# Spreading the router over the tiles of a window-attention + MoE kernel: two places a tile, one list product a part, an earlier second tile

## The chip, the core and the metric

One core of a Trainium2 chip runs the whole program. The metric is device time in microseconds, from the first to the last instruction of one execution plus what lies around it; lower is better. The engines are named as the profile names them: PE (TensorE matmul; PEld are its weight loads), DVE (VectorE), ACT (ScalarE), POOL (GpSimd), and SP, whose queue (SPq) issues most of the DMAs.

## What is computed

Attention over a window of 64 keys (8 batches, 8 heads, 576 positions, head size 64), and on its output a top-1 mixture of experts with a skip:

```
rel  = pos[:, None] - pos[None, :]
attn = softmax(where((rel >= 0) & (rel < 64), q @ k.T / 8, -1e9))
x    = (attn @ v) as [4608, 512]
do   = x @ w_skip > 0                      # other rows leave as x
e    = argmax(x @ w_gate); g = softmax(x @ w_gate)[e]     # 8 experts
out  = x + g * (relu(x @ w1[e]) @ w2[e])   # w1[e]: 512 x 1024
```

## The kernel before, in words

**Attention.** 36 tiles of 128 tokens go through a loop written out by hand (`for t in range(NT + 1)`, L868 to L894): inside `tc.manual_schedule()` every engine takes its instructions in program order. Turn t issues, in this order: loads that are due; `score(t+1)` (PE, L234); the gate matmuls of a coming v block (`gate_at`, PE and a copy on ACT); `soften(t)` (DVE: maximum L249, subtraction L250; then ACT: exponential L251); `tile_out(t-2)`, which is `av_tile` (PE L344, then on DVE the normalisation, L353 to L361) and two turns later a store; and `transpose_p(t-1)` (PE L260, ACT copy `ptm` L261). Scores sit in two PSUM buffers; the transposes, the gate matmuls and the router's own matmuls share another two (tag "t").

**Router.** Tiles are routed in groups of 8, 8, 6, 8, 4 and 2 (`GRP`). `route` is a generator: each `yield` ends a part. On DVE it reduces the logits (`lg`, L386), finds the winner (`gmx`, `gd`, `gfi`, `gfm`), builds a one-hot row (`goh`, `gohb`, after which it yields "sums"); then PE counts (`pr`, L410 and L413) and DVE goes on (`gds`, `base`, L422 and L423; `gnd`, `gs`, `gate`, `pos`, `low`, `posp`); then POOL writes one-hot positions (`hot`, L446), two tiles a part. `routes(n)` takes up to n parts; after "sums" it lets calls go by until the third, so that PE doesn't meet `gohb` too early. Before, a turn calls it at three places: ahead of `soften`, between normalisation and transposes, and after these (there with two parts from turn 22, `NCLOSE`, on).

**Lists.** When the third group is routed (22 tiles), `close_first` picks the two fullest experts, and `entries` makes their lists: DVE compares (`of`, L478), POOL multiplies it with five columns (`ofv`, L486, five products), PE sums (`pe`, L505), DVE turns it into indices (`entry`, L513 to L517), and POOL gathers the rows (`gather_x`, L524). The first item's rows are transposed (`split_x`, `px`, L684) in turns 32 and 33 (`XSPLIT`).

**Experts.** After the loop, `expert_chunk` issues one stretch of expert matmuls at a time (`up`: 12 matmuls and on ACT and DVE `hh`, `hl`; `down`: three wide matmuls a list tile and chunk; every fifth chunk is empty in the first items) and, ahead of it, the weight splits due (`whi` on ACT L647, `wlo` on DVE L648). While router parts are left, each chunk is followed by `routes(2)`. Then come `order_experts` (L952 on) and a loop that takes `PACE` parts of `late_lists` ahead of each chunk: `begins` (L969), then `entries` over nine steps of four tiles, with the matmuls (`peu`) two steps behind the products. Its list feeds the gather for the third item, whose transposes stand in the 29th chunk.

**Start.** SP loads q and k of the first two blocks, constants for the scores, `wg`, the first v (`load_v(0)`), q and k of blocks 2 and 3, the second q and k, and the router's constants (`load_constants`, `cf` and `cols`, with five small POOL instructions behind `cf`).

Of the kernel before, what the change touches and what calls it, by code (L numbers as in the profile page):

```python
# [13 lines left out]
ALU = mybir.AluOpType  # L14
# [5 lines left out]
P = 128  # L20
# [19 lines left out]
NCLOSE = 22  # L40
# [9 lines left out]
USPLIT = (35,)  # L50
RATE = 1

PACE = 4

XSPLIT = (32, 33)

# [68 lines left out]
def window_attention_moe(ctx: ExitStack, tc, a, out):  # L125
    nc = tc.nc
# [26 lines left out]
    vals = const.tile([P, 5, NT], BF16, name="vals")  # L153
# [31 lines left out]
    def load_qk(n, parts=((0, 4),)):  # L185
        b, g = divmod(n, 2)
        if parts[0][0] == 0:
            qs[n] = qkp.tile([P, 4, 4, 64], F32, name="q", bufs=NQB)
        q, k = qs[n], ks[n % NKB]
        for s, e in parts:  # L190
            s0 = s + 1 if s or not g else 0
            nc.sync.dma_start(k[:, s0 : e + 1], a["kT"][b, :, 4 * g + s0 - 1 : 4 * g + e])
            nc.sync.dma_start(q[:, s:e], a["qT"][b, :, 4 * g + s : 4 * g + e])
# [273 lines left out]
    def entries(ts, starts, le, pool, since, take, step, lag):  # L467


        nc_ = starts.shape[1]  # L470
        parts(slice(since, ts.stop))
        yield
        pe, built = None, []
        for t0 in range(ts.start, ts.stop, step):
            m = min(step, ts.stop - t0)
            tj = slice(t0, t0 + m)
            of = pool.tile([P, m, nc_], BF16, name="of", bufs=1 if take is psum else 3)
            nc.vector.tensor_tensor(  # L478
                of,
                posp[:, tj].unsqueeze(2).to_broadcast([P, m, nc_]),  # L480
                starts.unsqueeze(1).to_broadcast([P, m, nc_]),
                op=ALU.is_equal,
            )
            ofv = pool.tile([P, m, 5, nc_], BF16, name="ofv", bufs=1 if take is psum else 3)
            for v in range(5):
                nc.gpsimd.tensor_tensor(  # L486
                    ofv[:, :, v], of, vals[:, v, tj].unsqueeze(2).to_broadcast([P, m, nc_]), op=ALU.mult
                )
                if v in (1, 3):
                    yield  # L490
            built.append((t0, ofv))
            yield "sums" if take is psum else None
            if len(built) < lag and t0 + step < ts.stop:
                continue
            if pe is None:
                pe = (
                    psum.tile([P, 5, nc_], F32, name="pe", tag="t", bufs=2, padded_shape=[P, 5, 100])
                    if take is psum
                    else banks["late"].tile([P, 5, nc_], F32, name="peu", tag="u", bufs=1, padded_shape=[P, 5, 100])
                )  # L500
            while built and (len(built) >= lag or t0 + step >= ts.stop):
                first_t, ofs = built.pop(0)
                for j in range(ofs.shape[1]):
                    t = first_t + j
                    nc.tensor.matmul(pe, hot[:, t], ofs[:, j], start=t == ts.start, stop=t == ts.stop - 1)  # L505
                yield
        entry(pe, le, pool)
        yield
# [65 lines left out]
    held = [None, 0]  # L574

    def routes(n, sums=True):

        for _ in range(n):
            if not late:
                return  # L580
            if held[0] == "sums":
                held[1] += 1
                if not sums or held[1] < 3:
                    continue
            held[:] = next(late[0], late), 0
            if held[0] is late:
                late.pop(0)
# [52 lines left out]
    def weight_dma_first():  # L640
        weight_dma(ptr["dma"])
        ptr["dma"] += 1
# [189 lines left out]
    with tc.manual_schedule():  # L832
# [2 lines left out]
        nc.sync.dma_start(band, a["c_band"])  # L835
        load_qk(0, ((1, 2),))
        nc.sync.dma_start(ident, a["c_ident"])
        nc.sync.dma_start(wg, a["wg"])
        load_v(0)
        load_qk(0, ((2, 4),))  # L840
        load_qk(1)
        load_constants()
        at = {}

        def when_at(t, f, n):
# [22 lines left out]
        for t in range(NT + 1):  # L868
            m, r = divmod(t, 9)
            for f, n in at.get(t, ()):  # L870
                f(n)
            if t + 1 < NT:
                score(t + 1)
            for f, n in gate_at.get(t, ()):
                f(n)
            rest = its[0].split(*xhl[0], XSPLIT.index(t), "t") if t in XSPLIT else None
            routes(1)
            if t < NT:
                soften(t)
            if t >= 2 and t < NT:  # L880
                tile_out(t - 2)
            if rest is not None:
                rest()
            routes(1, False)
            if t >= 1 and t < NT:
                transpose_p(t - 1)
            routes(1 if t < NCLOSE else 2)
            for f, n, j in lower_at.get(t, ()):
                f(n, j)
            for _ in range(U0.count(t)):  # L890
                weight_dma_first()
            if t in USPLIT:
                weight_split(ptr["split"])
                ptr["split"] += 1  # L894
# [282 lines left out]
```

## Time and profile before

| | |
|---|---|
| median of 3 runs | 467.93 us (466.89 to 470.29) |
| the profiled execution | 465.82 us, span 464.0 us |
| busy share PE, DVE, ACT, POOL | 89%, 66%, 47%, 27% |
| mean granted TensorE clock | 0.975 of full |
| attention loop | to about 180 us |
| routing of the last groups and the late list, among the first expert chunks | about 183 to 238 us |
| rest of the experts | 238 to 464 us |

The shares are averages over stages with different limits: a busy PE near 89% includes 100 us in which it never rests and 32 us in which it rests a third of the time. How the stages stand is in the rows below.

### The profile page before, as it was taken

The numbers are of one execution on the slowest core, as the hardware profiler recorded it, in microseconds if no ns is written. First come the engines' busy times: TensorE is split into PE (matmuls) and PEld (weight loads), VectorE is DVE, ScalarE is ACT, GpSimd is POOL, SyncE is SP. The second block draws the span as 40 slices with busy tenths as digits, with TensorE's granted clock in tenths as the row PEclk, the third lists the DMA queues.
The fourth block names the chain that finished last, engine by engine and source line by source line (L and its number), as shares of the span: only waits on it lengthen the run. The fifth ranks groups of instructions, "written<-read, shape, count | busy, mean of one in ns | idle before, by whom it ended". The sixth has DMA issues, their size and how long they took to land.

```text
span 464.0 us, 11417 instructions
## 1 busy us (share of the span) xinstructions
PE 411.8 (89%) x4568; PEld 342.9 (74%) x4568; DVE 308.3 (66%) x609; ACT 218.4 (47%) x365; POOL 125.6 (27%) x188
## 2 busy tenths in 40 slices
PE   2899989979779967894899999999999999999983
PEld 2577767867567756783689888898888789988762
DVE  2478989989788988687533658947355566756420
ACT  1387667767546755462312534434243445444410
POOL 2311215116052505246860402405007030101010
PEclk9999999999898998996999999999999999999998
DMA  7999989949847943556533561845537456656100
GB/s 245 394 351 401 384 284 404 398 127 390 356 146 250 355 128 112 151 196 207 174 111 100 184 207 69 277 137 185 193 114 250 161 197 198 216 193 219 51 29 20
DMA packets 35096, 99.31 MB, mean 214 GB/s; under 512 B 4480, under 2 KB 6528, under 8 KB 35040
## 3 DMA queue, kind: packets, MB, share of 16 engines
q1 hardware_dynamic: 31840, 88.97, 55.8%
q0 software_dynamic: 3200, 9.58, 5.8%
q8 instruction: 37, 0.61, 0.5%
q14 instruction: 19, 0.16, 0.1%
HBM read 84.46 MB, written 14.39 MB: 213 GB/s over the span
## 4 chain that ended last, share of the span: by engine, by line
PE 64%; DVE 9%; ACT 3%; DMA 3%; POOL 2%; issue 1%; POOLq 0%; DVEq 0%; SPq 0%; ACTq 0%
PE p L695 8%; PE p L697 8%; PE p L696 8%; PE av L344 4%; PE yw L695 3%; PE yw L697 3%; PE yw L696 3%; PE yv L695 3%; PE yv L696 3%; PE yv L697 3%; PE pt L260 3%; PE ps L234 3%; POOL ofv L486 2%; DMA vm<-vp 2%; DVE s L250 2%; PE px L684 2%
## 5 line engine op out<-in xcount | busy, mean ns | idle before, releaser
L648 DVE TENSOR_TENSOR wlo<-raw,whi 128x1024 fp32r<-128x1024 f32 x72 | 88.1, 1229 | 15.4 <-ACT whi L647 15.4
L732 ACT ACTIVATE hh<-p 128x256 fp32r<-128x256 f32 (+6 forms) x72 | 27.7, 384 | 146.6 <-PE p L697 145.6
L697 PE MATMUL p<-xh,wlo 128*128 128x256 f32 (+6 forms) x288 | 84.2, 292 | 1.6 <-DVE wlo L648 1.6
L695 PE MATMUL p<-xh,whi 128*128 128x256 f32 (+6 forms) x288 | 85.3, 296 | 0.3 <-ACT ptm L261 0.3
L696 PE MATMUL p<-xl,whi 128*128 128x256 f32 (+6 forms) x288 | 84.1, 292 | 0.0
L733 DVE SCALAR_TENSOR_TENSOR hl<-p,hh 128x256 fp32r<-128x256 f32 (+6 forms) x72 | 30.3, 420 | 76.8 <-ACT hh L732 76.7
L647 ACT CAST whi<-raw 128x1024 fp32r<-128x1024 f32 x72 | 74.2, 1046 | 0.0
L755 POOL DMA_INDIRECT out<-yo,les x18 | 18.9, 1052 | 156.0 <-DVE yo L754 144.1
L695 PEld LDWEIGHTS p<-xh,whi 128*128 128x128 f32 x288 | 55.0, 191 | 3.4 <-ACT ptm L261 0.4
L251 ACT ACTIVATE s<-s 128x1024 f32<-128x1024 f32 x36 | 38.1, 1058 | 40.3 <-DVE s L250 38.1
L697 PEld LDWEIGHTS p<-xh,wlo 128*128 128x128 f32 x288 | 55.1, 191 | 2.0 <-DVE wlo L648 2.0
L696 PEld LDWEIGHTS p<-xl,whi 128*128 128x128 f32 x288 | 55.1, 191 | 1.4
L249 DVE TENSOR_REDUCE mx<-ps 128x8 f32<-128x1024 f32 x36 | 43.8, 1215 | 15.0 <-PE ps L234 15.0
L250 DVE TENSOR_TENSOR s<-ps,mx 128x1024 f32<-128x1024 f32 x36 | 44.1, 1225 | 5.1 <-PE pt L260 0.9
L260 PE MATMUL pt<-ident,s 128*128 128x128 f32 x288 | 41.0, 284 | 5.6 <-ACT ptm L261 5.6
L344 PEld LDWEIGHTS av<-vm,ptm 128*64 128x64 f32 x1024 | 36.1, 138 | 11.4 <-issue 5.7
L344 PE MATMUL av<-vm,ptm 128*64 128x74 f32 x1024 | 41.3, 233 | 2.2 <-ACT ptm L261 2.1
L315 POOL COPY vm<-vm 64x1184 f32<-64x1184 f32 x16 | 18.6, 1168 | 88.5 <-ACT vm L314 61.0
L234 PE MATMUL ps<-k,q 64*64 64x128 f32 x1024 | 37.3, 285 | 4.1 <-DMA q<-qT 4.1
L261 ACT COPY ptm<-pt 128x512 f32<-128x512 f32 x72 | 38.6, 580 | 4.7 <-PE pt L260 4.5
L260 PEld LDWEIGHTS pt<-ident,s 128*128 128x128 f32 x288 | 31.5, 143 | 9.8 <-ACT ptm L261 6.5
L234 PEld LDWEIGHTS ps<-k,q 64*64 64x64 f32 x1024 | 33.1, 142 | 7.2 <-DMA k<-kT 4.4
(173 smaller groups left out, 697.5 us busy)
## 6 DMA issues: line engine op xcount, KB each, us to landing
raw<-wq SPq DMA_DIRECT2D x72, 512.0 KB, 4.4
vm<-vp SPq DMA_DIRECT2D x16, 592.0 KB, 6.8
vT<-vT SPq DMA_DIRECT2D x16, 512.0 KB, 7.6
out<-x SPq DMA_DIRECT2D x32, 256.0 KB, 6.3
q<-qT SPq DMA_DIRECT2D x15, 512.0 KB, 9.0
k<-kT SPq DMA_DIRECT2D x8, 640.0 KB, 6.8
k<-kT SPq DMA_DIRECT2D x7, 512.0 KB, 8.3
kt<-kT SPq DMA_DIRECT2D x8, 256.0 KB, 7.6
```

What stands on the lines that cost most here:

```text
L234: nc.tensor.matmul(ps[64 * hf : 64 * hf + 64, r, p], q[h, p], k[h, :, p], start=False, stop=p == 3, skip_group_check=True,)
L249: nc.vector.tensor_reduce(mx, flat, axis=AX.X, op=ALU.max)
L250: nc.vector.tensor_tensor(s, flat, mx.unsqueeze(2).to_broadcast([P, 8, P]), op=ALU.subtract)
L251: nc.scalar.activation(s, s, AF.Exp, scale=0.125)
L260: nc.tensor.transpose(pt[:, p], s[:, 4 * r + p], ident)
L261: nc.scalar.copy(ptm[:, 4 * r : 4 * r + 4], pt)
L344: nc.tensor.matmul(av[64 * hf : 64 * hf + 64, h // 4, (h % 4) * VW : (h % 4 + 1) * VW], ptm[:, (h % 2) * 4 + h // 2, 64 * hf : 64 * hf + 6 ...
L647: nc.scalar.copy(hi, raw)
L648: nc.vector.tensor_tensor(lo, raw, hi.bitcast(F32), op=ALU.subtract)
L695: nc.tensor.matmul(o, lh, rh, start=first, stop=False)
L696: nc.tensor.matmul(o, lh, rl, start=False, stop=False)
L697: nc.tensor.matmul(o, ll, rh, start=False, stop=last)
```

## The change

The router is called at two places of a turn below turn 22: between softmax and normalisation, and after the transposes; from turn 22 on also ahead of the softmax. One call passes after "sums" where two did. The five products of a list step become one instruction over five times the elements, and the two `yield`s among them go, so that a step is two parts (products, matmuls) where it was four; `PACE` goes from 4 to 3. At the start, q and k of blocks 2 and 3 move ahead of `wg` and the first v, and the router's constants move to turn 2, behind the loads due there.

```
-PACE = 4
+PACE = 3
...
-            for v in range(5):
-                nc.gpsimd.tensor_tensor(
-                    ofv[:, :, v], of, vals[:, v, tj].unsqueeze(2).to_broadcast([P, m, nc_]), op=ALU.mult
-                )
-                if v in (1, 3):
-                    yield
+            nc.gpsimd.tensor_tensor(
+                ofv,
+                of.unsqueeze(2).to_broadcast([P, m, 5, nc_]),
+                vals[:, :, tj].rearrange("p v t -> p t v").unsqueeze(3).to_broadcast([P, m, 5, nc_]),
+                op=ALU.mult,
+            )
...
-                if not sums or held[1] < 3:
+                if not sums or held[1] < 2:
...
+        load_qk(0, ((2, 4),))
         nc.sync.dma_start(wg, a["wg"])
         load_v(0)
-        load_qk(0, ((2, 4),))
         load_qk(1)
-        load_constants()
...
+            if t == 2:
+                load_constants()
...
-            routes(1)
+            if t >= NCLOSE:
+                routes(1)
             if t < NT:
                 soften(t)
+            routes(1)
             if t >= 2 and t < NT:
                 tile_out(t - 2)
             if rest is not None:
                 rest()
-            routes(1, False)
             if t >= 1 and t < NT:
                 transpose_p(t - 1)
-            routes(1 if t < NCLOSE else 2)
+            routes(1)
```

## Rows read from the trace of the kernel before

**Rows 1.** Busy time of each engine by stretch (start and end, its length, then PE, PEld, DVE, ACT and POOL busy us with instructions, granted clock, DMA share, GB/s).

```profile
0.00:20.00 20.00, 9.91 (x125) 6.39 (x126) 4.92 (x5) 2.98 (x4) 4.52 (x17) 1.00 0.87 308
35.00:55.00 20.00, 20.00 (x435) 16.05 (x425) 18.07 (x31) 15.65 (x28) 2.92 (x3) 1.00 1.04 405
55.00:75.00 20.00, 16.87 (x351) 13.32 (x344) 17.97 (x43) 11.43 (x21) 5.42 (x8) 1.00 0.91 319
...
205.00:237.00 32.00, 22.18 (x146) 19.11 (x145) 21.01 (x51) 10.36 (x16) 23.81 (x54) 0.84 0.49 158
...
300.00:400.00 100.00, 100.00 (x593) 86.68 (x592) 55.86 (x77) 40.90 (x63) 18.65 (x16) 1.00 0.55 181
```

**Rows 2.** DVE's timeline, the subtractions of the softmax alone: turns 9, 13, 15, 16, 23 and 35 (start us, us, what).

```profile
51.60 1.23 DVE L250 TENSOR_TENSOR s<-ps,mx 128x1024 f32<-128x1024 f32 x1
...
71.64 1.22 DVE L250 TENSOR_TENSOR s<-ps,mx 128x1024 f32<-128x1024 f32 x1
...
79.16 1.23 DVE L250 TENSOR_TENSOR s<-ps,mx 128x1024 f32<-128x1024 f32 x1
82.84 1.23 DVE L250 TENSOR_TENSOR s<-ps,mx 128x1024 f32<-128x1024 f32 x1
...
113.92 1.23 DVE L250 TENSOR_TENSOR s<-ps,mx 128x1024 f32<-128x1024 f32 x1
...
177.91 1.23 DVE L250 TENSOR_TENSOR s<-ps,mx 128x1024 f32<-128x1024 f32 x1
```

**Rows 3.** DVE's timeline in turns 9 to 13: the first instruction of three runs of router parts and the maximum that follows each (in brackets the idle time before an instruction and what ended it).

```profile
54.42 0.75 DVE L386 TENSOR_REDUCE lg<-lh 128x72 f32<-128x576 f32 x1
...
56.12 1.21 DVE L249 TENSOR_REDUCE mx<-ps 128x8 f32<-128x1024 f32 x1
...
64.85 0.22 DVE L422 TENSOR_TENSOR gds<-pr,base 128x64 f32<-128x64 f32 x1 [0.87 <-PE pr L413]
...
65.40 1.22 DVE L249 TENSOR_REDUCE mx<-ps 128x8 f32<-128x1024 f32 x1
...
69.04 0.21 DVE L432 TENSOR_REDUCE gs<-gex 128x8 f32<-128x64 f32 x1
...
70.30 1.22 DVE L249 TENSOR_REDUCE mx<-ps 128x8 f32<-128x1024 f32 x1
```

**Rows 4.** Waits of the whole run: who waited for whom, us in total, times, longest.

```profile
PE pr L410 <- ACT ptm L261: 5.3, 3, 3.0
PE peu L505 <- POOL ofv L486: 9.8, 4, 6.9
```

**Rows 5.** The start: the gate matmuls of the second v on PE (timeline), and the router's constants among the DMA issues (count, KB each, median us to landing).

```profile
16.54 1.08 PE L294 MATMUL pw<-vT,wg 128*32 128x256 f32 x8 [1.73 <-DMA vT<-vT]
```

```profile
cf<-c_f SPq DMA_DIRECT2D x1, 181.0 KB, 7.5
cols<-c_col SPq DMA_DIRECT2D x1, 32.0 KB, 7.2
```

**Rows 6.** The first list: its last steps in the timeline, and the gathers among the DMA issues (median us from issue to landing).

```profile
149.78 0.17 DVE L513 COPY raw_e<-pe 128x20 f32<-128x20 f32 x1
150.64 1.25 POOL L524 DMA_INDIRECT xg<-out,es  x1 [6.13 <-DVE raw_e L516]
```

```profile
xg<-out,es POOLq DMA_INDIRECT x4, 7.5
```

**Rows 7.** DVE and PE among the expert chunks (timeline).

```profile
194.28 2.36 DVE L648 TENSOR_TENSOR wlo<-raw,whi 128x1024 fp32r<-128x1024 f32 x2
196.55 0.42 DVE L733 SCALAR_TENSOR_TENSOR hl<-p,hh 128x256 fp32r<-128x256 f32 x1
197.46 0.42 DVE L733 SCALAR_TENSOR_TENSOR hl<-p,hh 128x256 fp32r<-128x256 f32 x1 [0.50 <-ACT hh L732]
...
205.19 2.42 DVE L648 TENSOR_TENSOR wlo<-raw,whi 128x1024 fp32r<-128x1024 f32 x2 [0.30 <-ACT whi L647]
...
208.47 0.15 DVE L952 TENSOR_TENSOR c<-base,cf 128x8 f32<-128x8 f32 x1
...
211.61 1.21 DVE L648 TENSOR_TENSOR wlo<-raw,whi 128x1024 fp32r<-128x1024 f32 x1
...
213.12 0.23 DVE L478 TENSOR_TENSOR of<-posp,begins 128x72 bf16<-128x72 f32 x1
```

```profile
205.38 0.40 PE L695 MATMUL yw<-whi,hh 128*128 128x512 f32 x1
...
208.18 0.28 PE L695 MATMUL p<-xh,whi 128*128 128x256 f32 x1
```

**Rows 8.** The late list: POOL, PE and DVE (timeline).

```profile
213.52 6.80 POOL L486 TENSOR_TENSOR ofv<-of,vals 128x72 bf16<-128x72 bf16 x15 [4.50 <-DVE of L478]
...
231.47 1.36 POOL L486 TENSOR_TENSOR ofv<-of,vals 128x72 bf16<-128x72 bf16 x5 [0.31 <-DVE of L478]
234.21 1.11 POOL L524 DMA_INDIRECT xg<-out,les  x1 [1.38 <-DVE raw_e L516]
```

```profile
216.74 0.46 PE L505 MATMUL peu<-ofv,hot 128*128 128x90 bf16 x4 [6.91 <-POOL ofv L486]
```

```profile
233.25 0.25 DVE L513 COPY raw_e<-peu 128x90 f32<-128x90 f32 x1 [1.93 <-PE peu L505]
...
237.78 0.63 PE L684 MATMUL px<-ident,xg 128*128 128x128 f32 x4 [0.26 <-DMA xg<-out,les]
```

**Rows 9.** POOL's groups by form (count, busy us, mean ns of one, idle before).

```profile
L315 POOL COPY vm<-vm 64x1184 f32<-64x1184 f32 x16 | 18.6, 1168 | 88.5 <-ACT vm L314 61.0 <-issue 16.7 <-DMA k<-kT 10.7
L486 POOL TENSOR_TENSOR ofv<-of,vals 128x72 bf16<-128x72 bf16 x45 | 17.9, 434 | 5.9 <-DVE of L478 5.9
...
L463 POOL TENSOR_TENSOR left<-gate,vals 128x22 f32<-128x22 f32 x1 | 0.2, 233 | 0.1
```

## The prediction

> **What bounds the kernel now.** I read the stretches first. From 300 to 400 us PE never rests, and nothing of the change lies there; what can move lies ahead of 238 us [rows 1]. In the plain tiles (35 to 55 us) PE is full and DVE at 18.1 of 20 us; in the tiles with router parts (55 to 75 us) DVE stays at 18.0 and PE falls to 16.9: there DVE sets the pace [rows 1]. The distance between two subtractions shows the price: 3.68 us in a plain turn, but 71.64 - 51.60 = 20.04 us over the four turns that carry the first group, 5.3 us more than four plain ones [rows 2]. The runs of parts between take 1.70, 0.55 and 1.26 us, with some 0.4 us for `goh` and `gohb` 3.9 us; 0.87 us is DVE's wait for `pr` [rows 3], and the rest PE's delay behind that. `pr` is late because it follows the transposes and needs the PSUM slot that the copy `ptm` frees: 5.3 us on PE over three groups [rows 4].
>
> From 205 to 237 us PE does 22.2 of 32 us, at a granted clock of 0.84 [rows 1]. It waits 9.8 us for POOL's products [rows 4], 6.9 of them at the first list step [rows 8]. But POOL is not late by itself there: `of` came at 213.12 only, since DVE reached `order_experts` at 208.47 [rows 7], 3.1 us after PE had ended the chunk ahead of it (205.38).
>
> **Start.** The constants (181 + 32 KB) leave the front of the queue [rows 5]. PE's last wait of the start is for the second vT, at 16.54 us [rows 5]; at the 308 GB/s of this stretch [rows 1] 213 KB are 0.7 us, and this is what vT can gain: **-0.6**. The earlier q and k of blocks 2 and 3 let `score(1)` run sooner, but the first exponential stands on ACT behind the copy of that second gate matmul, so they bring nothing more; the other way, they put 512 KB ahead of the first vT, which still comes before the second. On POOL, `trib` now waits for `cf` in turn 2, with the copy of v block 2 (turn 3) behind it; its reader is `av_tile(4)` in turn 6, three plain turns (11 us) on, against a landing in 7.5 us [rows 5]: nothing. On SP the two issues stand ahead of turn 4's loads: nothing, or at worst 1 us once.
>
> **Tiles 9 to 23.** The parts of a group of 8, by counting calls: before 3, 3, 1, 3 and so on over four turns, all between a normalisation and the next maximum; after one or two a turn over six turns, half of them between softmax and normalisation. DVE does the same work. What goes is the wait: `pr` of groups 1 and 2 now stands on PE ahead of `av_tile`, which needs the same `ptm` copy anyway, and DVE comes to `gds` after a whole softmax. Six turns then cost 6 x 3.68 + 3.9 = 26.0 us; before, the same six cost 20.04 + 2 x 3.76 (71.64 to 79.16) = 27.6 [rows 2, 3]. With the second group taken alike and some loss where PE is full: **-2.5**. None of it, if PE's own 3.8 us a turn holds instead; that is the bound above.
>
> **Tiles 23 to 35.** These twelve turns take 64.0 us [rows 2], 19.8 over twelve plain ones. Parts by the same prices: rest of group 3 some 3.5, `close_first` and `of` 3.8, `entry` 0.9, group 4 4.0, two `xl` 1.4: 13.6, and some 6 of stalls. After, 1.2 us of group 4 (from `gs` on) falls behind the loop, and three stalls stay, each where DVE now meets PE ahead of the softmax: `pr` in turns 26 and 35 (1.2 each: score and gate matmul, then `ptm`'s slot, against DVE's normalisation) and `entry` in turn 31 behind `pe` (1.1). So 2.5 us of stalls go and 1.2 of work moves: 64.0 - 3.7, taken as **-3.5**; what the moved work costs later is in the waits among the chunks, below.
>
> **The first gather** moves from turn 29 to 31, two turns nearer to its transposes in turn 32. From `entry`'s start to the gather's issue are 0.9 us, from there to landing 7.5 in the median [rows 6], 3.6 for the late list (237.78 - 234.21 [rows 8]). PE comes to `px` about 5.3 us after `entry`'s start (`entry` 0.9, a softmax 2.4, score and gate matmul 2.0). So it waits 0 to 3, and ACT's next exponential, queued behind the copy of `px`, waits with it; the middle: **+1.5**.
>
> **Router parts among the chunks.** After the loop more is left: `order_experts` comes after chunk 19 where it came ahead of chunk 14 (counted), and one chunk stands between `gohb` and `pr` where two did. A chunk is 1.4 us: two end from 205.38 to 208.18 [rows 7]. Two splits and an `hl` (194.28 to 196.97) and the 1.7 of parts put `gohb` of group 5 at 198.7, where PE is done at about 197.05 (`hl` at 197.46 less ACT's 0.4) [rows 3, 7]: 1.6. For group 6: `hl` ends at 208.47, parts 0.75, PE there at 205.38 + 1.4: 2.4. **+4.0**; zero if DVE catches up before.
>
> **The late list.** A product of 360 elements: two-input products go from 233 ns at 22 elements to 1.36/5 = 272 at 72 with DVE quiet [rows 8, 9], 0.8 ns an element; the copy has 1 ns [rows 9]. So 0.5 to 0.6 us alone. Beside DVE's splits the small ones took 450 ns (15 in 6.80 [rows 8]), 1.7 times, so I take **1.0**; bounds 0.5 (fixed cost only saved) and 2.17 (five times 434 [rows 9], nothing saved).
> Counted from PE's end of the last chunk that DVE must finish: before, `px` of the third item starts 237.78 - 205.38 = 32.4 us later with 12 chunks of 1.4 in it: 15.6 us of lists and waits. After: `order_experts` at 2.9, `of` 4.65 later as before [rows 7] and one split of 1.2 more between (two chunks now stand there): 9. Product 1.0, PE there after 3 chunks: wait 5.9, less than 6.9. The nine steps then go with the chunks; the last two products leave together, and PE waits some 2.5 for them at the end. What is new: a chunk now stands ahead of `entry`, and DVE has its `hl` first, so `entry` starts 2.3 us after the last `peu` where it started at once; and only two chunks are left ahead of `px`, not three. Gather as before, 237.78 - 233.25 = 4.5 us from `entry`'s start [rows 8]: PE is there after 2.8 and waits 6.8 - 2.8 = 4.0 for it, where it waited 0.26. Total to `px` 27.2 with 8 chunks: 16.0 of lists and waits. **+0.4**, and **+0.5** for a lower clock after a wait of 4 us, as the 0.84 here shows [rows 1]. From `px` on, nothing changes.
>
> **Sum**, against the profiled execution of 465.8: -0.6 - 2.5 - 3.5 + 1.5 + 4.0 + 0.4 + 0.5 = -0.2. The median stands 2.1 higher; I give 467.8 beside 467.9. What the loop gains, the tail of the routing spends.
>
> **Rivals.**
> A, faster: the list stall goes. If DVE is not behind after chunk 18, `of` comes early, PE finds the products done, and the 9.8 us go [rows 4] while `pr` costs nothing: -6.6 + 1.5 (loop, gather) + 0 - 9.8 + 4.0 (`px`) = -10.9; half of it, the likelier size, 462. For: nine products in 9 us instead of 19. Against: `of` at 213.12 waited for DVE, not POOL, and the same splits stand there after.
> B, slower: the joined product costs what five did. From about 1.3 us each, POOL sets the list's pace again; at 2.17 nine are 19.5, the last at 9 + 19.5 where it was 20.5, +8: 476. For: the elements are the same. Against: 0.8 ns an element. A longer product could also lose a whole split each time: 0.58 + 1.22 = 1.8, nine 16.2, +5: 473.
> The Trainium skill ("SBUF — State Buffer", Who interferes with whom) has a DVE instruction with two SBUF inputs, as the splits are, hold the port that GpSimd reads through, for the whole instruction. The trace agrees in part: products beside splits took 450 ns, not 272, but fifteen got through in 6.8 us [rows 8]. By that rule 473 would come out; I give it 0.04 of B's chance.
> C, slower: at both `pr` among the chunks DVE has one more pair of splits ahead of `gohb` than I count, 2.4 us each [rows 7]: +4.8, 472.6 or more. It decides where the splits of a step (two each time) are issued after the parts and not before. For: DVE ran 3.1 us behind at 205.38. Against: one pair a step is all that is due until the order is known.
> D, the loop gains only the 0.87 at each `pr`, as DVE has the same work: +4 or so, 472, within the same 1%.
>
> **Chances.** Forecast and D 0.48; A 0.30; B 0.10; C 0.12. Within 1% (4.7 us, about what runs of this kernel can tell from no change) 0.48, faster 0.30, slower 0.22. The range leaves out the far ends of A and B: 460.5 to 474.0.
>
> **What would show it.** Subtractions of turns 9 to 15 at 26 us instead of 27.6; no wait of `gds` in turns 12 and 20, but one in 26 and 35; second vT at 16.0; `ofv` at 0.6 to 1.3 us; PE waiting for `gohb` twice among the chunks, for `ofv` some 8 us in all, and 4 us for the gather at the third item's `px`. Wrong if `ofv` is above 1.3 (B), or if `of` starts less than 6 us after PE's end of chunk 18 (A).

## The result, and the profile after

| | before | after |
|---|---|---|
| median of 20 runs, us | 468.3 | 471.1 |
| profiled execution: time, span, us | 465.8, 464.0 | 469.6, 467.8 |

The changed kernel is slower: ratio 1.0061, 95% interval 1.0041 to 1.0081. The time of 467.8 us and "no change" did not hold; the range did. (Disturbed runs, such as one of after at 590 us and one of e2 at 1354, are left out of the ratios.)

Three lengths tell where it went. The turn of a tile is told by its subtraction on DVE, here turns 9, 15, 23 and 35 of after, as in [rows 2]:

```profile
52.67 1.23 DVE L250 TENSOR_TENSOR s<-ps,mx 128x1024 f32<-128x1024 f32 x1
...
78.54 1.23 DVE L250 TENSOR_TENSOR s<-ps,mx 128x1024 f32<-128x1024 f32 x1
...
111.72 1.23 DVE L250 TENSOR_TENSOR s<-ps,mx 128x1024 f32<-128x1024 f32 x1
...
171.68 1.22 DVE L250 TENSOR_TENSOR s<-ps,mx 128x1024 f32<-128x1024 f32 x1
```

From turn 9 to turn 35 after takes 119.0 us where before took 177.91 - 51.60 = 126.3 [rows 2]: the loop gained 7.3. From there to the third item's transposes (`px` at 240.11, below; 237.78 in [rows 8]) it takes 68.4 us against 59.9, so the tail of the routing lost 8.6. From `px` to the end of the span it is 227.7 against 226.2: 1.5 more lost. With 1.1 us more before turn 9 that is the 3.8 us between the spans.

Inside the tail, PE's waits of after from 185 to 245 us (who waited for whom, total, times, longest; compare [rows 4]):

```profile
PE peu L505 <- POOL ofv L485: 8.4, 5, 6.5
PE pr L410 <- DVE gohb L407: 4.0, 2, 2.3
PE px L684 <- DMA xg<-out,les: 3.0, 1, 3.0
PE p L697 <- DVE wlo L648: 0.8, 1, 0.8
```

and after's stretches (start and end, length, then PE, PEld, DVE, ACT, POOL busy, granted clock, DMA share, GB/s), the first and the last beside those of [rows 1]:

```profile
55.00:75.00 20.00, 19.13 (x404) 15.07 (x405) 18.82 (x44) 13.41 (x25) 3.49 (x4) 1.00 0.95 342
...
185.00:205.00 20.00, 15.31 (x96) 13.72 (x95) 14.80 (x41) 9.06 (x16) 2.75 (x6) 0.91 0.46 140
205.00:242.00 37.00, 25.29 (x148) 22.13 (x148) 21.03 (x61) 9.49 (x14) 18.52 (x23) 0.79 0.44 145
```

The middle one was, in the kernel before:

```profile
185.00:205.00 20.00, 17.91 (x156) 15.86 (x155) 15.28 (x50) 8.84 (x17) 4.64 (x6) 1.00 0.57 182
```

In the loop PE is now busy 19.1 of 20 us where it was 16.9: the waits went, the work did not. Among the chunks the granted clock is 0.91 and then 0.79 where it was 1.00 and 0.84. What that means for a chunk is plain on PE's timeline of after, in the down product behind the second wait for `gohb` and in a later one:

```profile
205.17 0.17 PE L410 MATMUL pr<-gohb,trib 128*128 128x16 bf16 x1 [2.31 <-DVE gohb L407]
...
205.94 0.63 PE L697 MATMUL yw<-whi,hl 128*128 128x512 f32 x1
...
206.36 0.63 PE L695 MATMUL yw<-whi,hh 128*128 128x512 f32 x1
...
211.34 0.39 PE L696 MATMUL yw<-wlo,hh 128*128 128x512 f32 x1
```

The granted clock of these two stretches of after (length, PE busy, granted clock, DMA share, GB/s):

```profile
205.20:208.90 3.70, 3.70 (x15) 0.56 0.44 157
209.10:215.30 6.20, 6.20 (x43) 1.00 0.21 63
```

Behind the wait the same matmul takes 0.63 us, at the lower of the two levels (1.2 GHz; granted clock 0.56), and 0.39 at the higher (2.4 GHz; 1.00). The late list and the gather of after, on POOL, DVE and PE, as in [rows 7, 8]:

```profile
219.97 5.25 POOL L485 TENSOR_TENSOR ofv<-of,vals 128x360 bf16<-128x360 bf16 x4 [10.54 <-DVE of L478]
227.05 2.60 POOL L485 TENSOR_TENSOR ofv<-of,vals 128x360 bf16<-128x360 bf16 x2 [1.83 <-DVE of L478]
229.88 2.38 POOL L485 TENSOR_TENSOR ofv<-of,vals 128x360 bf16<-128x360 bf16 x3 [0.23 <-DVE of L478]
```

```profile
215.99 0.17 DVE L963 TENSOR_SCALAR order<-key 128x8 int32<-128x8 f32 x1
...
235.79 0.24 DVE L513 COPY raw_e<-peu 128x90 f32<-128x90 f32 x1
```

```profile
221.96 0.46 PE L505 MATMUL peu<-ofv,hot 128*128 128x90 bf16 x4 [6.48 <-POOL ofv L485]
...
240.11 1.12 PE L684 MATMUL px<-ident,xg 128*128 128x128 f32 x4 [3.04 <-DMA xg<-out,les]
```

What one joined product takes is hidden in these sums. All nine (ns: shortest, median, longest; first and last start), then two of them and the two splits that began beside them:

```profile
L485 POOL TENSOR_TENSOR ofv<-of,vals x9: 816/824/1934, 220.0 to 231.4; 128x360 bf16<-128x360 bf16 x9
```

```profile
219.97 1.93 POOL L485 TENSOR_TENSOR ofv<-of,vals 128x360 bf16<-128x360 bf16 x1 [10.54 <-DVE of L478]
...
222.64 0.82 POOL L485 TENSOR_TENSOR ofv<-of,vals 128x360 bf16<-128x360 bf16 x1
```

```profile
220.00 1.22 DVE L648 TENSOR_TENSOR wlo<-raw,whi 128x1024 fp32r<-128x1024 f32 x1
...
222.69 1.85 DVE L648 TENSOR_TENSOR wlo<-raw,whi 128x1024 fp32r<-128x1024 f32 x1
```

Six of the nine take 0.82 us. The other three take 1.81 to 1.93: each ran beside a split (1.22 us) and lost nearly its length. Two splits that began during a product of 0.82 us were the ones to lose: they take 1.85 and 1.68 us. PE waits as long for the first one as before (6.5 for 6.9), and now also for the gather; the transposes behind that wait take 1.12 us where before they took 0.63 [rows 8].

### The profile page after: what moved, and what is told of

Read it like the earlier page. It is cut to its first block, busy times and chain, and to the rows that moved or that the text cites. A ratio compares the mean times of both kernels' runs of the same rounds, so it can differ in the third digit from the quotient of the medians.

```text
span 467.8 us, 11368 instructions
## 1 busy us (share of the span) xinstructions
PE 413.1 (88%) x4568; PEld 345.2 (74%) x4568; DVE 306.4 (66%) x609; ACT 217.6 (47%) x365; POOL 113.8 (24%) x148
## 4 chain that ended last, share of the span: by engine, by line
PE 53%; DVE 6%; DMA 3%; ACT 2%; issue 2%; POOL 1%; POOLq 0%; SPq 0%; ACTq 0%; DVEq 0%
PE p L695 8%; PE p L697 8%; PE p L696 8%; PE yw L695 4%; PE yw L697 4%; PE yw L696 4%; PE yv L695 3%; PE yv L696 3%; PE yv L697 3%; PE px L684 2%; DVE wlo L648 2%; PE yu L696 2%; PE yu L697 2%; PE yu L695 2%; DMA xg<-out,es 1%
## 5 line engine op out<-in xcount | busy, mean ns | idle before, releaser
L695 PE MATMUL p<-xh,whi 128*128 128x256 f32 (+6 forms) x288 | 87.0, 302 | 0.1
L697 PE MATMUL p<-xh,wlo 128*128 128x256 f32 (+6 forms) x288 | 85.8, 298 | 0.8 <-DVE wlo L648 0.8
L696 PE MATMUL p<-xl,whi 128*128 128x256 f32 (+6 forms) x288 | 85.8, 298 | 0.0
L695 PEld LDWEIGHTS p<-xh,whi 128*128 128x128 f32 x288 | 56.9, 198 | 3.2 <-ACT whi L647 0.2
L696 PEld LDWEIGHTS p<-xl,whi 128*128 128x128 f32 x288 | 57.0, 198 | 1.5
L697 PEld LDWEIGHTS p<-xh,wlo 128*128 128x128 f32 x288 | 56.9, 198 | 1.0 <-DVE wlo L648 1.0
L234 PE MATMUL ps<-k,q 64*64 64x128 f32 x1024 | 36.1, 279 | 0.5 <-DMA q<-qT 0.5
```

The lines of the kernel that those rows point to most:

```text
L234: nc.tensor.matmul(ps[64 * hf : 64 * hf + 64, r, p], q[h, p], k[h, :, p], start=False, stop=p == 3, skip_group_check=True,)
L695: nc.tensor.matmul(o, lh, rh, start=first, stop=False)
L696: nc.tensor.matmul(o, lh, rl, start=False, stop=False)
L697: nc.tensor.matmul(o, ll, rh, start=False, stop=last)
```

## The experiments

**Theory**: the places gain in the loop what the trace says, and the tail loses it, by the waits for `gohb` and the gather and by chunks at the lower clock behind each wait. **Rivals**: the start or the joined product is what costs; or the tail gives back whatever the loop gains. The lengths come from each kernel's trace as above (turn 9 to 35, turn 35 to the third item's `px`, `px` to the end, us); ratios are against the kernel before on the same chip, whose median was 468.3 to 470.2 us by chip. Each version has twelve runs, e14 seven, e6, e17 and e18 six.

| kernel | 9 to 35 | 35 to `px` | `px` to end | median | ratio, 95% |
|---|---|---|---|---|---|
| before | 126.3 | 59.9 | 226.2 | 468.3 | |
| after | 119.0 | 68.4 | 227.7 | 471.1 | 1.0061 [1.0041, 1.0081] |
| e1_start | 129.3 | 59.9 | 226.3 | 470.8 | 1.0007 [0.9973, 1.0041] |
| e2_lists | 132.4 | 61.2 | 226.3 | 474.0 | 1.0058 [1.0029, 1.0087] |
| e3_after_old_start | 120.8 | 70.0 | 229.0 | 471.6 | 1.0037 [1.0007, 1.0067] |
| e4_more_parts | 123.4 | 64.8 | 226.2 | 470.3 | 1.0014 [0.9984, 1.0043] |
| e5_filled | 120.9 | 65.6 | 227.7 | 468.0 | 0.9949 [0.9916, 0.9982] |
| e6_five_products | 120.8 | 73.4 | 227.8 | 477.5 | 1.0164 [1.0118, 1.021] |
| e7_loop_low | 122.3 | 64.8 | 227.6 | 468.3 | 0.9958 [0.9922, 0.9993] |
| e8_later_sums | 119.7 | 65.9 | 227.8 | 468.5 | 0.9955 [0.9926, 0.9984] |
| e9_before_filled | 130.8 | 58.5 | 226.3 | 468.1 | 1.0007 [0.9971, 1.0044] |
| e10_hold_three | 119.7 | 65.4 | 227.6 | 469.0 | 1.0017 [0.9984, 1.0051] |
| e11_filled_later | 120.7 | 64.5 | 229.2 | 468.4 | 1.0003 [0.9976, 1.003] |
| e12_late_joined | 128.4 | 61.2 | 226.3 | 469.4 | 1.0021 [0.999, 1.0052] |
| e13_after_again | 119.6 | 68.6 | 227.7 | 471.2 | 1.0052 [1.0025, 1.008] |
| e14_px_filled | 119.2 | 68.8 | 228.0 | 471.2 | 1.0095 [1.006, 1.013] |
| e15_hold_later_filled | 120.0 | 61.8 | 229.7 | 467.2 | 0.9993 [0.9967, 1.0019] |
| e16_pr_filled | 121.4 | 65.3 | 227.7 | 469.8 | 1.0055 [1.0022, 1.0088] |
| e17_filled_once | 119.8 | 61.7 | 226.2 | 463.3 | 0.988 [0.9833, 0.9928] |
| e18_hold_later | 123.3 | 61.5 | 229.2 | 464.6 | 0.9883 [0.9839, 0.9928] |

**The parts of the change.** e1: the kernel before with the start's order alone (q and k ahead of `wg` and v, constants in turn 2).

> Only the start of the change on the kernel before: q and k of blocks 2 and 3 ahead of wg and the first v, router constants in turn 2. Theory 1 (read from the trace of after): the first gate matmul runs earlier, frees vT's slot, so the loads of the third v and of q and k are issued about 3 us earlier and share the bandwidth with the second vT, which lands 0.5 us later; the constants in turn 2 then make the vT of turn 4 late by another 0.6. So about +1.1 us by the subtraction of turn 9 (52.6 against 51.6), and a ratio of about 1.002. Theory 2 (the prediction): the constants leave the queue ahead of the second vT, -0.6 us (51.0).

No difference. e3 is the changed kernel with the start of before:

> The changed kernel with the start of before. Theory 1: it gets back the 1.1 us of the start and keeps the rest, +2 us against before (ratio 1.003 to 1.005), the subtraction of turn 35 near 170.6. If start and loop don't add up (the load queue is full in both), it stays at the changed kernel's 1.006.

No difference either: 471.6 and 471.1. With either start, turn 9 begins anywhere between 51.2 and 53.8 us in single profiles; the 1.1 us of after's one profile are that.

e2: the kernel before with both lists joined, and the pace that goes with it; e12: the late list alone.

```diff
-            for v in range(5):
-                nc.gpsimd.tensor_tensor(ofv[:, :, v], of, vals[:, v, tj]...)
-                if v in (1, 3):
-                    yield
+            nc.gpsimd.tensor_tensor(ofv, of..., vals[:, :, tj]..., op=ALU.mult)
...
-    PACE = 4
+    PACE = 3
```

> Only the lists of the change on the kernel before: one product a step, PACE 3; router places and start as before. Theory 1: DVE, not POOL, is late at the first step, so the wait for the first product stays near 5 to 6 us, the later waits for products go, entry comes with 8 chunks left ahead of px, so no wait there: the transposes of the third item come 2 to 4 us earlier, ratio 0.992 to 0.996. Theory 2: POOL was the bound and all 9.8 us go: 0.979 to 0.983. Theory 3: the joined product costs what five did (2.2 us) and nothing changes: 1.000.

> The kernel before with the joined product and pace 3 in the late list alone; the first list keeps its five products with parts between them, and places, hold and start are as before. With both lists joined, the ratio was 1.006 and the tiles from turn 28 on had lost 5 us. Theory that those 5 us are the first list's, whose sums and entry then stand in one turn behind the transposes: turn 35 as before (no loss in the tiles), ratio 0.996-1.001. Rival, the joined late list costs the time itself: turn 35 as before, the third item's transposes 3 to 6 us later after turn 35, ratio 1.004-1.008.

e2 missed: alone, the lists make the kernel before slower by as much as the whole change. Its tail is only 1.3 us longer, as e12's; what it loses is the loop, 132.4 us. Its turns 23 to 31 take 46.7 us, 41.9 to 42.5 in the other kernels that have these places. There the first list's sums now stand behind the transposes of the turn that also holds its entry, and PE waits 1.9 us for the `ptm` copy ahead of `pe`. e12 leaves the loop in the spread of the kernel before (126.3 to 130.8) and its ratio includes 1. Its joined product takes 1.37 us in the mean, as there five of the nine waited for a split, in after three. So nothing is won by joining in the old places; e6 shows what it is worth in the new ones.

e6: the changed kernel with five products, but no part between them.

```diff
-            nc.gpsimd.tensor_tensor(ofv, of..., vals[:, :, tj]..., op=ALU.mult)
+            for v in range(5):
+                nc.gpsimd.tensor_tensor(ofv[:, :, v], of, vals[:, v, tj]...)
```

> The changed kernel with the five products of a list step again in place of the joined one, but without parts between them, so that every other instruction stands where the changed kernel has it. Measured so far: 0.43 us for one of five of 72 elements (2.2 us for a step) against 0.8-1.3 us for the joined one of 360. Theory that the joined product by itself is the cheaper and is not what costs the time: each of nine steps is 0.9-1.4 us longer on GpSimd, the wait for the first `ofv` grows from 6.5 to 7.5 us, the third item's transposes come 2 to 8 us later, ratio to before 1.010-1.022. Rival, joined is no cheaper beside VectorE: ratio 1.003-1.008 as the changed kernel.

6.4 us slower than after by the medians, 4.8 by the ratios, and the wait for the first `ofv` is 7.0 us. By POOL's groups five took 5 x 374 = 1,870 ns a step, the joined one 1,163. The joined product is not the cost; it is worth some 5 us of tail.

e7: the new places and hold in tiles 0 to 21 only, the rest as before.

```diff
-                if not sums or held[1] < 3:
+                if not sums or held[1] < (2 if progress[0] < NCLOSE - 2 else 3):
...
-            routes(1)
+            if t >= NCLOSE:
+                routes(1)
             if t < NT:
                 soften(t)
+            if t < NCLOSE:
+                routes(1)
...
-            routes(1, False)
+            if t >= NCLOSE:
+                routes(1, False)
```

> The kernel before with the changed kernel's places for the parts (one behind the softmax instructions, one behind the transposes, none in front) and its hold of one call in tiles 0 to 21 alone; from tile 22 on, the lists, the pace and the start as before. Theory that the places gain and the lists and what follows lose: turn 23 begins 2-4 us earlier than before, the gain arrives at the end in full, ratio 0.991-0.996. Rival, the tail gives back whatever the loop gains (a fixed distance to the weights or the lists): turn 23 earlier, ratio 0.998-1.002.

Faster, at the slow end of the range. Turns 9 to 23 take 59.1 us, as in every kernel with the new places, against 62.3 to 64.0 with the old. The tail is 4.9 us longer than that of before all the same, with 3.1 us for the gather and 1.3 for `gohb`: part of the gain is given back even with the old parts.

e4: two parts behind the transposes from turn 22 on (with the old start), so that the order comes after chunk 13.

```diff
-            routes(1)
+            routes(1 if t < NCLOSE else 2)
```

> The changed kernel with the start of before and, from turn 22 on, two router parts after the transposes instead of one, so that the order of the experts is due after chunk 13 as before and not after chunk 19. Theory 1: the loop's gain (7 us in the changed kernel) is mostly kept, some of it given back where close_first is in one run again (5 us left), and the tail costs no more than before, since gohb and pr stand two calls apart in a chunk less often late, and entry comes 8 chunks ahead of px: -6 to -9 us, ratio 0.981 to 0.987. Rival: the loop's gain came from fewer parts a turn and not from their place, so it goes: 0.995 to 1.002.

A miss. The order came early and the list's wait grew: 10.8 us for `ofv`, 8.1 of them at once, as the first sums start 11.1 us behind PE's end of the chunk ahead of the order (217.92 - 206.85). Before it was 216.74 - 205.38 = 11.4 [rows 7, 8], after 221.96 - 211.11 = 10.9: the lag is VectorE's and about the same in the three, and here only two chunks of work stand in it. So it isn't enough to bring the order forward.

**Waits and clock in the tail.** e5 to e18 are the changed kernel, except e9, the kernel before. Extra bf16 matmuls in front of a waiting one write the PSUM tile that the real one then overwrites; they do nothing but keep PE at work.

```diff
+            for _ in range(90):
+                nc.tensor.matmul(pe, hot[:, 0], hot[:, 1, : 5 * nc_]..., start=True, stop=True)
```

> The changed kernel with extra bf16 matmuls (18 of 128 columns in front of each of the last two `pr`, 90 of 90 columns in front of the first `peu` product, 25 of 128 columns in front of the third item's transposes) that write the same PSUM tile before its real first matmul overwrites it, so that TensorE works where it now waits (1.7 + 2.3 us for `gohb`, 6.5 us for the first `ofv`, 3.0 us for the gather). Theory that some 3 to 4 us of the change's missing gain are the chunks run at the lower clock level: the clock of 205 to 242 us goes from 0.79 to 0.9 or more, a down product of six falls from 2.6 to 1.4-2.0 us, and the ratio to the kernel before falls from 1.006 to 0.998-1.003. Rival, the clock's price is hidden behind the waits for the lists: the clock rises, the ratio stays at 1.005-1.008 or grows by the filler that runs past the waits.

> The kernel before with 90 extra bf16 matmuls of 90 columns in front of its first `peu` product (its 6.9 us wait for the first `ofv`), written into the tile that the real product then overwrites. The changed kernel went from 1.006 to 0.995 of the kernel before with such matmuls in its four long waits. Theory that the change itself lost by the lower clock: the kernel before has fewer chunks at the lower level (yw at 1.4 us for six, not 2.6), so it gains less, 0.5 to 2 us, ratio 0.996-0.999. Rival, both kernels pay alike for the wait: gain of 4 to 5 us, ratio 0.989-0.992, and the clock explains nothing of the difference between the two.

> The changed kernel with 18 extra matmuls of 128 columns in front of each of the last two `pr` alone (its waits of 1.7 and 2.3 us for gohb). Theory that a chunk's clock falls behind these two waits: clock of 185-215 us at 1.0 instead of 0.87-0.91, 1 to 2 us faster than the changed kernel up to the first `peu`, of which the wait for `ofv` gives back nothing or half. Rival, VectorE sets the pace from there to the first `ofv`: the clock rises, the first `peu` comes at the same distance behind turn 35 (50.3 us), time as the changed kernel.

> The changed kernel with 30 extra matmuls of 128 columns in front of the third item's transposes alone (its 3.0 us wait for the gather). The changed kernel's profile has its end 227.7 us behind these transposes, the kernel before 226.2, and the transposes and chunks there at the lower clock. Theory that the 1.5 us is the lower clock after this wait: the clock of 240-245 us rises to 1.0, six yv or yw at 1.4 us, the end comes 226.2-226.6 us behind the transposes, 1.0-1.5 us faster than the changed kernel. Rival, the distance is the gather's own lateness (the second gather and what follows): 227.5-228 us as before, same time as the changed kernel.

e5's windows of PE (length, PE busy, granted clock):

```profile
185.00:205.00 20.00, 17.34 (x151) 1.00 0.49 160
205.00:245.00 40.00, 32.86 (x299) 0.91 0.44 145
```

The clock rose from 0.91 and 0.79 to 1.00 and 0.91, the tail became 2.8 us shorter, the median 3.1, and the intervals of the two ratios lie apart. In e9 the clock rose too (205 to 245 us: 0.96, before 0.87) and its tail is 1.4 us shorter than that of before, but its time did not move by what can be measured: this speaks for a lower clock that costs the changed kernel more. In e16, 18 matmuls ahead of each of the two `pr`:

```profile
192.79 1.17 PE L412 MATMUL pr<-hot 128*128 128x128 bf16 x18
194.50 0.18 PE L414 MATMUL pr<-gohb,trib 128*128 128x32 bf16 x1 [0.54 <-DVE gohb L407]
...
204.25 1.18 PE L412 MATMUL pr<-hot 128*128 128x128 bf16 x18
206.71 0.17 PE L414 MATMUL pr<-gohb,trib 128*128 128x16 bf16 x1 [1.27 <-DVE gohb L407]
```

`gohb` comes no earlier, but the chunks behind it run at the higher level (185 to 215 us at 1.00), and the tail is 3.1 us shorter in the profile. In the medians that is 1.4 us, in the ratios nothing (1.0055; after has 1.0052 on the same chip, e13), so by itself it is not shown to shorten the run. e14 missed, by its own edit: the 30 matmuls ran a second time in front of a later item's transposes.

```profile
240.65 0.65 PE L687 MATMUL px<-ident,xg 128*128 128x128 f32 x4 [1.86 <-DMA xg<-out,les]
...
324.11 1.85 PE L685 MATMUL px<-hot 128*128 128x128 bf16 x30
325.79 0.61 PE L687 MATMUL px<-ident,xg 128*128 128x128 f32 x4
```

The transposes do run at the higher level (0.65 us, not 1.12) and the next are 1.4 us nearer, but at 324 us PE waits for nothing and the second run costs 1.7. e5, e11 and e15 carry the same ballast (1.4, 1.4 and 3.4 us).

e8 moves the first sums one chunk back; e10 holds two calls among the chunks, as before; e11 is e5 (with 60 matmuls, not 90, ahead of the first `peu`) with e8.

```diff
-            for _ in range(PACE):
+            for _ in range(pace.pop(0) if pace else PACE):      # e8: pace = [3, 3, 3, 0, 4, 4, 4, 4]
...
-                if not sums or held[1] < 2:
+                if not sums or held[1] < (3 if progress[0] > NT - 2 else 2):      # e10
```

> The changed kernel with the late list's parts per chunk 3, 3, 3, 0, 4, 4, 4, 4 in place of 3 each: the first `peu` product stands one chunk later on TensorE (behind the chunk it now stands in front of), the last where it was. Theory that the 6.5 us wait for the first `ofv` is a fixed lag of VectorE less the chunks that stand between: the wait falls to 4-5 us, the list ends 1-2 us earlier, ratio 1.000-1.004. Rival, what is taken from this wait comes back at the later products or at the gather (3.0 us before the third item's transposes): ratio 1.005-1.008.

> The changed kernel with its hold of one call in the tiles and of two calls among the chunks, as in the kernel before: the last two `pr` stand one chunk later on TensorE, one pair of parts later. The two waits for `gohb` (1.7 and 2.3 us) go. Theory that they are paid in full and with them a chunk each at the lower clock: 3 to 5 us faster than the changed kernel, ratio 0.995-1.000. Rival, the order and the lists come a chunk later and the wait for the first `ofv` or for the gather grows by what the two waits gave: ratio 1.004-1.008.

> Two edits that each made the changed kernel faster, together: the extra matmuls (18 in front of the last two `pr`, 60 in front of the first `peu`, 25 in front of the third item's transposes) and the late list's parts 3, 3, 3, 0, 4, 4, 4, 4 by chunk. Theory that one takes the lower clock and the other a wait, so that they add: ratio 0.986-0.991. Rival, both act by the same thing (fewer chunks at the lower clock): ratio 0.993-0.996 as each alone.

e8: the wait for the first `ofv` fell to 5.1 us and the list ended earlier (16.0 us from `order` to `raw_e`, not 19.8): 2.5 us of tail. e10: the waits for `gohb` fell from 4.0 to 1.4 us, and 3.0 us of tail came of it, but the wait for the gather rose to 5.2. PE is idle as long in this tail as in after's (20.0 and 19.8 us); the 3.0 us are busy time of the same matmuls (45.4 for 48.6, at a granted clock of 0.87 for 0.85). What ends the tail then is the chain of order, nine steps, entry and gather. e11 did not add; without its ballast of 1.4 us it would be near 467, an estimate.

> The changed kernel itself, on the same chip as the three that follow. Theory: its distance to the kernel before is the change's and holds on any chip, ratio 1.004-1.008, median 470.5-472. Rival, the distance differs with the chip by as much as itself: ratio 0.997-1.002 or above 1.010.

471.2 us on another chip: on these two the changed kernel's time is the same. e5, e7, e8 and e15 are faster than it by intervals that lie apart from both of its own; those of e4, e10 and e11 touch them.

> The changed kernel with the hold of two calls among the chunks, the late list's parts 3, 3, 3, 0, 4, 4, 4, 4, and extra matmuls in front of the first `peu` (60 of 90 columns) and the third item's transposes (60 of 128 columns). Theory that each takes another piece of the tail (the waits for gohb, one for ofv, the lower clock): turn 35 to the third item's transposes 61 to 64 us instead of 68.4, end 226.2-226.6 behind them, 4 to 6 us faster than the changed kernel, ratio to before 0.992-0.998. Rival, once PE's own waits are gone the list's chain (order, nine steps, entry, gather) ends the tail, as the gather wait of 5.2 us with the hold alone suggests: 64.5-66 us, 2 to 3 us faster than the changed kernel as each edit alone.

> The same order of parts without any extra matmul: hold of two calls among the chunks, and the late list's parts 3, 3, 3, 0, 4, 4, 4, 4. Theory that the waits carry the most of the tail's loss and the clock the rest: 2 to 4 us faster than the changed kernel (467-469 us, ratio 0.996-1.000), and 2 to 4 us slower than with the extra matmuls, by the chunks at the lower level behind the waits for ofv and the gather, and 1.4 us behind the transposes. Rival, the extra matmuls bring nothing but the clock's look in the trace: within 1 us of the version with them.

> The version with the hold of two calls among the chunks, the late list's parts 3, 3, 3, 0, 4, 4, 4, 4 and the extra matmuls in front of the first `peu` and of the third item's transposes, now without their second run at 318 us, which took 3.4 us in its profile. Theory: its end comes 226.2 us behind the third item's transposes as in the kernel before (229.7 with the second run), 3.4 us faster: 463.5-464.5 us, ratio to before 0.988-0.994. Rival, the 3.4 us were hidden in part: 465.5-467, ratio 0.994-1.000.

Hold and pace together, without any extra matmul (e18), give a tail of 61.5 us: 6.9 of the 8.6 are back. With the two filled waits and no ballast (e17) it is no shorter, as the gather ends it, but the stretch behind `px` falls from 229.2 to 226.2. The windows of PE from 235 to 245 us (length, busy, granted clock) and the transposes, of e18 and then e17:

```profile
235.00:245.00 10.00, 7.82 (x30) 0.58 0.37 100
```

```profile
237.35 1.11 PE L684 MATMUL px<-ident,xg 128*128 128x128 f32 x4 [2.18 <-DMA xg<-out,les]
244.94 0.42 PE L684 MATMUL px<-ident,xg 16*128 16x16 f32 x4
```

```profile
235.00:245.00 10.00, 10.00 (x68) 1.00 0.20 58
```

```profile
233.67 0.61 PE L693 MATMUL px<-ident,xg 128*128 128x128 f32 x4
238.37 0.42 PE L693 MATMUL px<-ident,xg 16*128 16x16 f32 x4
```

Two pairs of transposes with the same chunks between are 7.6 us apart at a clock of 0.58 and 4.7 at 1.00. In after they are 6.2 apart, so 2.9 us is the far end of what this wait costs: e18's profiled run is its slowest (468.25 us). Both kernels beat before and after, at 463.3 and 464.6 us (six runs each); the 1.3 us between them are inside the intervals.

## Why the prediction was wrong

**Start, -0.6**: nothing (e1, e3). The second vT landed no sooner in after (PE's gate matmul at 17.0 us, [rows 5] has 16.5). In e1 that matmul stands at 16.0, as forecast, and the median did not move; single profiles spread by more than the term.

**Tiles 9 to 23, -2.5**: 25.9 us for turns 9 to 15 where 26.0 was said, and -3.3 in all, in nearly every profile. `gds`, which waited 0.87 and 0.80 us for `pr` in these tiles, waits no more, and waits 1.00 and 0.61 us in turns 26 and 35, as forecast. **Tiles 23 to 35, -3.5 and +1.5 for the gather**: together -4.0 in the pair of profiles; the gather cost 0.8 us of wait. Right in kind, some 2.8 us too small in all.

**`pr` among the chunks, +4.0**: 1.7 and 2.3 us, as worked out, and e10 takes 2.6 of it away again. **The joined product, 1.0 us**: 1.16 in the mean, below the 1.3 of rival B, and near 1.0 by luck, as both prices behind it were off. Where it waits for no split the product takes 0.82 us where 0.5 to 0.6 was said. Beside a split the forecast read the mean of the small ones (450 ns) as a slow-down of 1.7; by single instructions they take 0.30 us, and 1.13 to 1.36 where one waited for a split. The joined product too pays nearly a whole split when it waits for one (1.81 to 1.93 us; rival B's second price had 1.8), but three of nine did so, not all, and 473 did not come. The Trainium skill ("SBUF — State Buffer", Who interferes with whom) has a VectorE instruction with two SBUF inputs and a GpSimd instruction that reads SBUF lock each other out. The trace agrees within some 0.2 us: of a split's 1.22 us the three products lost 1.0 to 1.1, and the two splits, begun when a product had 0.77 and 0.60 us to go, lost 0.63 and 0.46. First wait 5.9, measured 6.5; wait at `px` 4.0, measured 3.0. Rival A is out, as `of` starts 8.5 us (219.57 - 211.11) after PE's end of the chunk ahead of the order, not under 6; C is out, as both waits for `gohb` have the forecast length.

The step that failed is **"+0.5 for a lower clock"**, with **"From `px` on, nothing changes"**. From PE's first expert matmul behind the loop to the third item's transposes, and from these to the next ones, both kernels run the same matmuls. PE in these two stretches (length, PE busy, granted clock, DMA share, GB/s), of before and then of after:

```profile
183.11:237.78 54.67, 41.84 (x312) 0.91 0.50 160
237.78:242.51 4.73, 4.73 (x28) 1.00 0.52 162
```

```profile
176.93:240.11 63.18, 45.79 (x310) 0.85 0.45 146
240.11:246.29 6.18, 6.18 (x29) 0.75 0.43 117
```

The first stretch holds all that the tail lost: 8.5 us. (From turn 35 to that first matmul it is 5.2 us before and 5.3 after, though PE waits 2.3 us for `ptm` there.) Of the 8.5 us, 4.6 are waits (idle 17.4 us, before 12.8): 4.0 for `gohb` and 2.8 more for the gather, less 1.4 at `ofv` and 0.8 at `wlo`. That is close to the 4.0 + 0.4 that the sum had for them. The other 3.9 are busy time of the same matmuls at a lower granted clock, and behind `px`, where PE doesn't rest in either kernel, 1.5 follow: 5.4 us where 0.5 was said. Each new wait was priced by its length alone; each also puts the chunk behind it at half the clock (granted 0.54 and 0.56 behind the two for `gohb`, 0.50 behind the gather's). In all the tail and what follows lost 10.1 us where 4.9 was said; with 1.7 more from the start and 2.8 less from the loop, that is about the 4.0 us between the sum of -0.2 and the 3.8 of the two profiles. So the sum came as near as it did by luck in part: what the loop gained beyond the forecast hid half of what the clock cost.

What the runs do not settle is how much of the clock's 5.4 us counts in the time of the whole run. e5 got some 3 us of median back by raising the clock, with 1.4 us of ballast in it; e14 and e16, with one kind of wait filled each, got nothing that can be measured, and e17 gained 1.3 us on e18, inside the intervals. Where PE runs into the list's chain again (e17 against e18, up to `px`), a faster chunk only waits longer.

The loop takes 126.3 to 130.8 us in four kernels that have it unchanged. Most of that spread lies in its last four turns. Turns 31 to 35 (all engines as in [rows 1]), of before, e1 and e9:

```profile
155.81:177.91 22.10, 16.05 (x313) 12.87 (x309) 19.91 (x44) 13.45 (x25) 7.03 (x12) 1.00 0.58 202
...
155.74:180.45 24.71, 17.98 (x316) 14.38 (x310) 19.93 (x44) 13.77 (x25) 7.03 (x12) 0.93 0.48 169
...
159.55:184.15 24.60, 18.55 (x314) 14.87 (x310) 19.91 (x44) 13.57 (x25) 7.03 (x12) 0.86 0.49 170
```

and of after and e18:

```profile
151.06:171.68 20.62, 16.71 (x329) 13.68 (x324) 17.49 (x36) 13.42 (x24) 4.25 (x5) 1.00 0.61 202
...
150.95:175.83 24.88, 19.46 (x327) 15.73 (x322) 17.49 (x36) 13.40 (x24) 4.24 (x5) 0.85 0.53 168
```

DVE does the same work in the same time; where the granted clock is lower, PE is busy longer and the turns are up to 4.3 us longer. What lowers it in one execution and not in another is open. The profile of before had the shortest loop of its four, so the loop's real gain is nearer 8 than 7 us: 5.8 in turns 9 to 31, where the profiles mostly agree, the rest uncertain.

## What to carry to other kernels

When work leaves a loop for the tail behind it, price the tail's waits twice: their length, and the work behind them at the lower clock, up to where PE next waits anyway. Find the chain that ends the tail (here order, list, entry, gather) and change its order as well as the loop's: the same change with one more call held and the list's first sums a chunk later went from 0.6% slower to 1.2% faster. An extra matmul in a wait is a cheap probe for the clock, but look in the trace where else it runs.

## What the hardware showed beyond that

After a wait of 2.2 to 5.2 us for the gather TensorE came back at the lower level. From the third item's transposes to the next ones PE then took 6.1 to 6.3 us in seven kernels and 7.5 to 7.6 in two (e3, e18), at granted clocks of 0.60 to 0.76, and 4.7 us at 1.00 in every kernel without that wait. With matmuls in the wait whose results are thrown away it took 4.7 to 4.8 too (e5, e14, e15, e17; in e11, at 0.73, it did not help). So the wait cost 1.4 to 2.9 us more after it had ended, and not by its length: that of 5.2 us (e10) cost 1.4, that of 2.2 (e18) 2.9.

Where a product on GpSimd and a split on VectorE met, one of them waited: a product of 0.82 us took 1.81 to 1.93, or a split of 1.22 took 1.68 to 1.85. So a mean over products says little without how many of them waited. And the loop, unchanged, differs by up to 4.5 us between executions, most of it where the granted clock differs.
